# Sliding local attention beside a gated MLP: block 0's z2 from centred x, a 3 to 1 weight split, and later due times for the output

## The chip, the cores and the metric

The kernel runs on one core of a Trainium2 chip. A core has TensorE (PE in the profile, with its weight loads as PEld), VectorE (DVE), ScalarE (ACT), GpSimd (POOL) and SyncE (SP). SyncE and ScalarE issue most DMAs, each on its own queue. The metric is the device time of one execution, the median of the runs, in microseconds (us); lower is better.

## The reference

The input is x, 2048 tokens of 512 features in bf16. A layer norm without gain or bias gives xn, and the output is x + A(xn) + B(xn).

```python
# A: 32 heads of 16, each query sees 8 keys, 2 tokens apart, itself the last
qkv  = xn @ wqkv
attn = softmax(mask(q . k[pos - 2*w] * 0.25), over w = 0..7)
A    = (sum_w attn * v[pos - 2*w]) @ wo
# B: gated MLP that mixes tokens; w_in is 512 x 1792
z    = gelu(xn @ w_in)            # two halves of 896: z1 and z2
z2   = layernorm(z2)
g    = w_sp @ z2 + b_sp           # w_sp is 2048 x 2048, over tokens
B    = (z1 * g) @ w_out
```

## The kernel before

**A planner.** The kernel does not write instructions straight out. It adds tasks (`T` and `dma` call `Plan.add`, line 54), each with an engine, the buffers it reads and writes, a guessed duration and a name. `Plan.schedule` (line 95) then plays the tasks through on these guesses and so fixes one order per engine. Among the tasks that can start first it takes the one with the better priority and then the one added earlier; most of the attention's VectorE work has the lower priority `FILL`. A DMA is taken to last its bytes over a bandwidth, and to be usable a fixed latency later (`dma_lat`, 1700 ns, used at line 193). A task can have a margin: it is not taken before its inputs' planned end plus that margin. Output blocks have 1500 ns (line 983). The tasks then run on the chip in the planned order on each engine, with semaphore waits for what they depend on. The plan only sets the order; how long things take is up to the chip.

`plan.orders` (line 1010) writes part of the order by hand: in each list, the named tasks of an engine must start in this sequence.

**The head.** Tokens are in 16 blocks of 128. For a block, `ln_block` (line 594) takes statistics on VectorE (`bnst` line 598, `bnag` line 601), the inverse root of the variance on GpSimd (`rstd`, line 603), and normalises on VectorE (`norm`, line 605). The first four blocks are transposed by TensorE against an identity (`xTr`, line 620) and copied out of PSUM by ScalarE (`xTe`, lines 626 and 634); for block 0 VectorE copies the second half (`xTf`, line 630). Later blocks are transposed by a DMA (`xTd`, line 609). While x and the first weights are loading, TensorE runs matmuls on zeros (`warm` and `fill0`, line 570): nine of 512 columns, and later two of 320.

`z2_block` (line 777) multiplies one block with the second half of w_in, 448 columns at a time (`z2_b_hf`, line 785, four matmuls over the 512 features), and ScalarE takes the gelu and its row sums (`z2g`, line 790). These weights come in four DMAs (`ld_win_h`, line 541): `w_in2a` and `w_in2b` are the first and second 448 columns, each cut into two halves of the features, one on SyncE's queue and one on ScalarE's.

**The middle.** Per group of 512 tokens: Q and K (`qk_pair`, line 665, ScalarE's copy line 673), V to DRAM (line 647), the products of queries and shifted keys and their sums on VectorE (lines 689 and 694), a DMA transposition (line 706), sums within a head (714, 717) and the softmax. Meanwhile TensorE does z2 and z1 (line 802).

**The end.** TensorE forms g in 28 groups of 16 matmuls (`g_group`, line 908), with w_sp transposed by DMA (`ld_wT`, line 841). VectorE multiplies each by z1 (line 915), and between these does the attention's sum over values (`pv_pair`, lines 933, 937, 941), on V rows gathered by a DMA on ScalarE's queue (line 925). Each pair's result is transposed by a DMA on SyncE's queue (`OTd`, line 946). There are two pairs to a group of 512 tokens. `out_block` (line 956) fills a PSUM bank with x, adds the attention's product with wo (line 974) and the MLP's with w_out (line 978), and stores the result (copy line 987, DMA line 990).

Of the kernel before, what the change touches and what calls it, by code (L numbers as in the profile page):

```python
# [14 lines left out]
class Plan:  # L15
# [79 lines left out]
    def schedule(self, lookahead=64, slack=120.0, dma_bw=300.0, xbar_bw=190.0,  # L95
# [37 lines left out]
        while remaining:  # L133
# [52 lines left out]
            if t.dma is not None:  # L186
# [6 lines left out]
                t.end = max(xe, st + iss) + dma_lat  # L193
# [115 lines left out]
    warm=9,  # L309
    fill0=2,  # L310
# [4 lines left out]
def build_kernel(nc, A_x, A_wqkv, A_wo, B_x, B_w_in, B_w_sp, B_b_sp, B_w_out, out, report=False, sched_kw=None,  # L315
# [79 lines left out]
    with ExitStack() as es:  # L395
# [68 lines left out]
        R("xnT0a", "sb", [(off["xnT"] + dc * S, off["xnT"] + dc * S + 128) for dc in range(2)])  # L464
        R("xnT0b", "sb", [(off["xnT"] + dc * S, off["xnT"] + dc * S + 128) for dc in range(2, 4)])
# [5 lines left out]
        for nm, lo, hi, h0, h1 in (("w_in1", 0, FH, 0, 4), (("w_in2a", 0), FH, FH + HF, 0, 2),  # L471
                                   (("w_in2a", 1), FH, FH + HF, 2, 4), (("w_in2b", 0), FH + HF, 2 * FH, 0, 2),
                                   (("w_in2b", 1), FH + HF, 2 * FH, 2, 4)):
            R(nm, "sb", [(off["w_in"] + dc * 1792 + lo, off["w_in"] + dc * 1792 + hi) for dc in range(h0, h1)])
# [23 lines left out]
        def dma(eng, fn, nbytes, chan, reads=(), writes=(), name="", xbar=False, prio=None):  # L498
            return T(eng, fn, reads=tuple(reads), writes=tuple(writes), name=name, prio=prio,
                     dma=dict(chan=chan, nbytes=nbytes, xbar=xbar))  # L500
# [40 lines left out]
        def ld_win_h(nm, lo, n):  # L541
            for h in range(2):
                dma(("sp", "act")[h], (lambda h: lambda e: e.dma_start(
                    AC(off["w_in"] + lo + 2 * 1792 * h, [[1792, 2], [1, n]]),
                    B_w_in[256 * h: 256 * h + 256, lo: lo + n].rearrange("(c p) n -> p c n", p=128)))(h),
                    256 * n * 2, (nm, h), writes=[(nm, h)], name="ld%s_%d" % (nm, h))
# [3 lines left out]
        ld_win_h("w_in2a", FH, HF)  # L550
        ld_win_h("w_in2b", FH + HF, HF)
        ld_x(2, "sp")
        ld_x(3, "act")
        for which, eng in ((0, "sp"), (1, "sp")):
# [3 lines left out]
                512 * 512 * 2, ("wqk", which), reads=[("w_in2a", 0)],  # L558
                writes=[(("wq", "wk")[which], c) for c in range(4)],
                name="ld%s" % ("qk"[which]))  # L560
        for b in range(4, min(8, NB)):
            ld_x(b, "sp", after=[("w_in2a", 0)])
# [31 lines left out]
        def ln_block(b):  # L594
# [10 lines left out]
            T("dve", lambda v: v.tensor_scalar(A("xn", 512, 512 * sl), xin, Fv("mv", 1, 2 * b),  # L605
                                               Fv("rstd", 1, b), ALU.subtract, ALU.mult),
              reads=[("xin", xs_), ("mv", b), ("rstd", b)], writes=[("xn", sl)], est=400, name="norm%d" % b)
            if b >= XDMA:
                dma("sp", lambda e: e.dma_start_transpose(AC(off["xnT"] + 128 * b, [[S, 4], [1, 128]]),
                                                          A("xn", 512, 512 * sl)),  # L610
                    128 * 512 * 2, ("xT", sl), reads=[("xn", sl)], writes=[("xnT", b)], name="xTd%d" % b, xbar=True)
                return
            k = next_bank()
            k2 = next_bank() if b == 0 else k

            def tr(t):
                last = None
                for dc in range(4):
                    kk = k if dc < 2 else k2
                    last = t.matmul(ps[:, 512 * kk + 128 * dc: 512 * kk + 128 * dc + 128],  # L620
                                    A("xn", 128, 512 * sl + 128 * dc), ident, start=True, stop=True)
                return last
            T("pe", tr, reads=[("xn", sl), "ident"], writes=[("ps", k), ("ps", k2)], est=4 * c_mm(128),
              name="xTr%d" % b)
            if b == 0:
                T("act", lambda a: a.activation(AC(off["xnT"] + 128 * b, [[S, 2], [1, 128]]),  # L626
                                                ps[:, 512 * k: 512 * k + 256].rearrange("p (c n) -> p c n", c=2),
                                                ACTF.Copy),
                  reads=[("ps", k)], writes=["xnT0a"], est=c_act(256), name="xTe%d" % b)
                T("dve", lambda v: v.tensor_copy(AC(off["xnT"] + 2 * S + 128 * b, [[S, 2], [1, 128]]),  # L630
                                                 ps[:, 512 * k2 + 256: 512 * k2 + 512].rearrange("p (c n) -> p c n", c=2)),
                  reads=[("ps", k2)], writes=["xnT0b"], est=c_dve(256), name="xTf%d" % b)
            else:
                T("act", lambda a: a.activation(AC(off["xnT"] + 128 * b, [[S, 4], [1, 128]]),
                                                bank(k).rearrange("p (c n) -> p c n", c=4), ACTF.Copy),
                  reads=[("ps", k)], writes=[("xnT", b)], est=c_act(512), name="xTe%d" % b)
            if b == 0:
                filler(cfg["fill0"], "fill0", 160.0 * cfg["fill0"], reads=("zeros", ("xn", 0)), w=320)
# [138 lines left out]
        def z2_block(b):  # L777
            for hf in range(2):
# [3 lines left out]
                def mm(t, k=k, c0=c0):  # L782
                    last = None
                    for dc in range(4):
                        last = t.matmul(ps[:, 512 * k: 512 * k + HF], AC(off["xnT"] + dc * S + 128 * b, [[1, 128]]),  # L785
                                        AC(off["w_in"] + 1792 * dc + c0, [[1, HF]]), start=(dc == 0), stop=(dc == 3))
                    return last
                T("pe", mm, reads=[("xnT", b), (("w_in2a", "w_in2b")[hf], 0), (("w_in2a", "w_in2b")[hf], 1)], writes=[("ps", k)],
                  est=4 * c_mm(HF), name="z2_%d_%d" % (b, hf))
                T("act", (lambda k, hf: lambda a: a.activation(  # L790
                    A("z2", HF, FH * b + HF * hf), ps[:, 512 * k: 512 * k + HF], ACTF.Gelu_apprx_tanh,
                    accum_out=Fv("s1", 1, 2 * b + hf)))(k, hf),
# [276 lines left out]
```

## Time and profile before

| | us |
|---|---|
| median of 3 runs (lowest, highest) | 236.54 (236.46, 236.55) |
| profiled execution, its own time | 238.13 |
| span of that execution, first to last instruction | 236.3 |
| TensorE busy in the span | 230.9 (98%) |
| VectorE busy | 202.8 (86%) |
| ScalarE busy | 117.6 (50%) |
| GpSimd busy | 51.8 (22%) |

A line of the timeline has the start and the length in us, the engine, the source line and operation, what is written and read, how many instructions were merged, and in brackets the idle time before and who ended it. A q after an engine's name (SPq) means the issuing of a DMA, not its transfer. A line of the waits has who waited for whom, the total in us, how often, and the longest. A line of the chain of work has a start, a length and what ran. The view of one source line gives durations in ns and, for DMAs, the time from issue to landing in us.

### The profile page before, as it was taken

How to read it: one execution, taken by the hardware profiler on the slowest of the kernel's cores; microseconds unless marked ns; L12 is line 12 of the kernel's file. 1: busy time of each engine (PE TensorE's matmuls, PEld its weight loads, DVE VectorE, ACT ScalarE, POOL GpSimd, SP SyncE). 2: the span in 40 equal slices, each digit the busy share in tenths (PEclk: the TensorE clock that was granted, in tenths of full speed). 3: DMA queues.
4: the chain of work that ended last, by engine and by line, in shares of the span. 5: the costliest groups of instructions: out<-in, count | busy, mean ns of one | idle time of the engine just before them, and what ended most of it. 6: DMA issues, size and time to landing. Idle time of an engine off the chain costs nothing.

```text
span 236.3 us, 2933 instructions
## 1 busy us (share of the span) xinstructions
PE 230.9 (98%) x1094; PEld 109.9 (47%) x1094; DVE 202.8 (86%) x230; ACT 117.6 (50%) x227; POOL 51.8 (22%) x67
## 2 busy tenths in 40 slices
PE   8999999999999999999999999999999799999995
PEld 2454454554554444444444444444444344444553
DVE  4789969998989989997999991799999999999900
ACT  2798488988988978942012132134124134111441
POOL 4447963771690050001301000001000000000000
DMA  6999986290209899696549999999773959912132
GB/s 226 281 356 189 206 223 192 92 178 0 90 3 178 202 249 260 116 247 214 147 96 242 199 215 232 248 182 337 191 206 93 243 147 275 223 23 44 67 89 67
DMA packets 87021, 41.75 MB, mean 177 GB/s; under 512 B 66000, under 2 KB 85856, under 8 KB 87008
## 3 DMA queue, kind: packets, MB, share of 16 engines
q1 hardware_dynamic: 70928, 23.24, 48.4%
q10 hardware_dynamic: 14640, 14.13, 20.4%
q0 software_dynamic: 1440, 4.21, 6.6%
q8 instruction: 8, 0.13, 0.2%
q14 instruction: 5, 0.04, 0.0%
HBM read 20.05 MB, written 5.26 MB: 107 GB/s over the span
## 4 chain that ended last, share of the span: by engine, by line
DVE 50%; PE 31%; DMA 9%; POOL 5%; issue 2%; ACT 2%; DVEq 0%
DVE arena L689 11%; DVE arena L694 9%; DMA arena<-arena 9%; PE ps L908 9%; PE ps L978 6%; DVE arena L933 6%; DVE arena L937 4%; DVE arena L915 4%; POOL fpool L831 4%; PE ps L974 4%; PE ps L665 4%; PE ps L647 3%; PE ps L785 3%; DVE arena L834 2%; DVE arena L717 2%
## 5 line engine op out<-in xcount | busy, mean ns | idle before, releaser
L908 PE MATMUL ps<-arena 128*128 128x512 bf16 x448 | 97.5, 379 | 0.0
L908 PEld LDWEIGHTS ps<-arena 128*128 128x128 bf16 x448 | 43.9, 98 | 52.8 <-ACT ps L902 0.2
L902 ACT ACTIVATE ps<-arena 128x512 f32<-128x512 bf16 x28 | 16.5, 599 | 62.2 <-DVE arena L915 62.1
L933 DVE TENSOR_TENSOR arena<-arena 128x4096 bf16<-128x4096 bf16 x16 | 36.3, 2285 | 0.4
L689 DVE TENSOR_TENSOR arena<-arena 128x4096 bf16<-128x4096 bf16 x16 | 36.1, 2285 | 0.2
L937 DVE TENSOR_TENSOR arena<-arena 128x4096 bf16<-128x4096 bf16 (+1 forms) x16 | 28.1, 1754 | 0.3
L665 PE MATMUL ps<-arena 128*128 128x512 bf16 x128 | 28.3, 379 | 0.0
L694 DVE TENSOR_TENSOR arena<-arena 128x4096 bf16<-128x4096 bf16 x12 | 27.5, 2288 | 0.2
L978 PE MATMUL ps<-arena 128*128 128x512 bf16 (+2 forms) x119 | 27.0, 366 | 0.0
L785 PE MATMUL ps<-arena 128*128 128x448 bf16 x128 | 25.5, 353 | 0.2 <-DVE arena L630 0.2
L802 PE MATMUL ps<-arena 128*128 128x512 bf16 x112 | 24.3, 379 | 0.0
L665 PEld LDWEIGHTS ps<-arena 128*128 128x128 bf16 x128 | 14.5, 113 | 13.1
L915 DVE TENSOR_TENSOR arena<-ps,arena 128x512 bf16<-128x512 f32 x28 | 19.1, 680 | 0.0
L673 ACT ACTIVATE arena<-ps 128x1024 bf16<-128x1024 f32 x16 | 16.3, 1021 | 5.3 <-PE ps L665 4.9
L987 ACT ACTIVATE arena<-ps 128x512 bf16<-128x512 f32 (+1 forms) x16 | 9.4, 585 | 18.4 <-PE ps L978 17.0
L790 ACT ACTIVATE arena<-ps 128x448 bf16<-128x448 f32 x32 | 17.3, 542 | 2.4
L978 PEld LDWEIGHTS ps<-arena 128*128 128x128 bf16 x119 | 13.2, 113 | 11.3
L974 PE MATMUL ps<-arena 128*128 128x512 bf16 (+2 forms) x68 | 16.6, 366 | 1.6 <-DMA arena<-arena 1.6
L785 PEld LDWEIGHTS ps<-arena 128*128 128x128 bf16 x128 | 12.3, 98 | 12.0 <-ACT arena L626 0.7
L807 ACT ACTIVATE arena<-ps 128x512 bf16<-128x512 f32 x28 | 15.9, 595 | 3.2 <-PE ps L802 2.7
L802 PEld LDWEIGHTS ps<-arena 128*128 128x128 bf16 x112 | 10.9, 98 | 13.2
L679 POOL COPY arena<-arena 128x16 bf16<-128x16 bf16 x12 | 14.4, 1207 | 10.9 <-DVE arena L689 9.2
(61 smaller groups left out, 191.2 us busy)
## 6 DMA issues: line engine op xcount, KB each, us to landing
arena<-vscr ACTq DMA_DIRECT2D x8, 1152.0 KB, 7.5
arena<-in_A_x_dram ACTq DMA_DIRECT2D x17, 128.0 KB, 6.0
vscr<-arena POOLq DMA_DIRECT2D x16, 128.0 KB, 2.3
arena<-in_A_x_dram SPq DMA_DIRECT2D x15, 128.0 KB, 4.6
out_dram<-arena ACTq DMA_DIRECT2D x15, 128.0 KB, 1.9
arena<-in_A_wqkv_dram SPq DMA_DIRECT2D x3, 512.0 KB, 5.4
ascr<-arena POOLq DMA_DIRECT2D x4, 256.0 KB, 4.1
arena<-ascr POOLq DMA_DIRECT2D x4, 256.0 KB, 3.5
```

What stands on the lines that cost most here:

```text
L665: last = t.matmul(bank(k + which), AC(off["wqk"] + 1024 * dc + col0, [[4, 128]]), AC(off["xnT"] + dc * S + 512 * j, [[1, 512]]), start=(dc ...
L689: T("dve", lambda v: v.tensor_tensor(pbv, qb, kb, ALU.mult), reads=[("QT", c, j), ("KT", c, j), ("KTpad", c, j)], writes=[("pb", s_)], est ...
L694: T("dve", lambda v: v.tensor_tensor(A("pb", 4096, 4096 * a), A("pb", 4096, 4096 * a), A("pb", 4096, 4096 * b), ALU.add), reads=[("pb", b) ...
L785: last = t.matmul(ps[:, 512 * k: 512 * k + HF], AC(off["xnT"] + dc * S + 128 * b, [[1, 128]]), AC(off["w_in"] + 1792 * dc + c0, [[1, HF]]) ...
L790: T("act", (lambda k, hf: lambda a: a.activation(A("z2", HF, FH * b + HF * hf), ps[:, 512 * k: 512 * k + HF], ACTF.Gelu_apprx_tanh, accum_ ...
L802: lastm = t.matmul(bank(k), AC(off["w_in"] + 1792 * dc + 128 * fc, [[1, 128]]), AC(off["xnT"] + dc * S + 512 * j, [[1, 512]]), start=(dc = ...
L908: last = t.matmul(bank(k), AC(off["z2"] + FH * sh + 128 * fc, [[1, 128]]), AC(off["wT"] + WSL * r_ + sh * 512, [[1, 512]]), start=False, s ...
L915: T("dve", lambda v: v.tensor_tensor(uv, bank(k), uv, ALU.mult), reads=[("ps", k)], writes=[("z1T", fc, tc)], est=c_dve(512) + 20, name="u ...
L933: T("dve", (lambda iv, tv, av: lambda v: v.tensor_tensor(tv, iv, av, ALU.mult))(iv, tv, av), reads=[("attn", j), ("Ve", par)], writes=[("V ...
L937: T("dve", (lambda n: lambda v: v.tensor_tensor(AC(off["Vs"], [[4096, 2], [1, n]]), AC(off["Vs"], [[4096, 2], [1, n]]), AC(off["Vs"] + n, ...
L974: t.matmul(po, AC(off["OT"] + 512 * ot_pos(tb) + 128 * cc, [[1, 128]]), AC(off["wo"] + 512 * cc + c0, [[1, n]]), start=False, stop=False, ...
L978: last = t.matmul(po, AC(off["z1T"] + fc * S + t0, [[ts, 128]]), AC(off["w_out"] + 512 * fc + c0, [[1, n]]), start=False, stop=(fc == FC - ...
```

## The change

Block 0: VectorE only subtracts the mean from x, in two halves of 256 features (`ctr0`, `ctr1`). TensorE transposes the halves, ScalarE copies both out, and z2 of block 0 is computed from them in two steps of two matmuls each. The inverse root is applied later, as the scale of ScalarE's gelu. The normalised block 0, which Q, K, V and z1 still need, is now computed on GpSimd and transposed by a DMA on SyncE's queue.

Loads: `w_in2a` is cut 3 to 1 over the features, with three quarters on ScalarE's queue and one on SyncE's. x block 2 goes ahead of `w_in2b` on SyncE's queue. x blocks 4 and 5 now follow the Q and K weights, and these follow block 0's transposition.

Written orders: on VectorE the statistics of block 2 now come before the normalisation of block 1 (they came after); GpSimd gets a list. Warm-up matmuls go from nine to seven and the filler's from two to one.

Planner: a DMA can have a latency of its own, 3400 ns for the V rows and 3600 ns for the attention's transpositions (1700 before), and the margin of output blocks goes from 1500 to 2500 ns.

```diff
-                t.end = max(xe, st + iss) + dma_lat
+                t.end = max(xe, st + iss) + t.dma.get("lat", dma_lat)
...
-    warm=9,
-    fill0=2,
+    warm=7,
+    fill0=1,
...
-        def ld_win_h(nm, lo, n):
-            for h in range(2):
-                dma(("sp", "act")[h], (lambda h: lambda e: e.dma_start(
-                    AC(off["w_in"] + lo + 2 * 1792 * h, [[1792, 2], [1, n]]),
-                    B_w_in[256 * h: 256 * h + 256, lo: lo + n].rearrange("(c p) n -> p c n", p=128)))(h),
-                    256 * n * 2, (nm, h), writes=[(nm, h)], name="ld%s_%d" % (nm, h))
+        def ld_win_h(nm, lo, n, cut, h):
+            c0, c1 = (cut, 4) if h == 0 else (0, cut)
+            dma(("sp", "act")[h], lambda e: e.dma_start(
+                AC(off["w_in"] + lo + 1792 * c0, [[1792, c1 - c0], [1, n]]),
+                B_w_in[128 * c0: 128 * c1, lo: lo + n].rearrange("(c p) n -> p c n", p=128)),
+                128 * (c1 - c0) * n * 2, (nm, h), writes=[(nm, 1 - h)], name="ld%s_%d" % (nm, h))
...
-        ld_win_h("w_in2a", FH, HF)
-        ld_win_h("w_in2b", FH + HF, HF)
+        for h in range(2):
+            ld_win_h("w_in2a", FH, HF, 3, h)
         ld_x(2, "sp")
+        for h in range(2):
+            ld_win_h("w_in2b", FH + HF, HF, 2, h)
...
+            if b == 0:
+                for h in range(2):
+                    T("dve", (lambda h: lambda v: v.tensor_scalar(A("attn", 256, 256 * h), xin[:, 256 * h: 256 * h + 256],
+                                                                  Fv("mv", 1, 2 * b), None, ALU.subtract))(h),
+                      reads=[("xin", xs_), ("mv", b)], writes=[("xc", h)], est=270, name="ctr%d" % h)
+            T("pool" if b == 0 else "dve", lambda v: v.tensor_scalar(A("xn", 512, 512 * sl), xin, Fv("mv", 1, 2 * b),
                                                Fv("rstd", 1, b), ALU.subtract, ALU.mult),
...
-            if b >= XDMA:
+            if b >= XDMA or b == 0:
                 dma("sp", lambda e: e.dma_start_transpose(AC(off["xnT"] + 128 * b, [[S, 4], [1, 128]]),
...
+                    T("pe", trh, reads=[("xc", h), "ident"], writes=[("ps", k)], est=2 * c_mm(128), name="xTr0%d" % h)
+                    T("act", (lambda h, pt: lambda a: a.activation(A("attn", 256, 512 + 256 * h), pt, ACTF.Copy))(h, pt),
+                      reads=[("ps", k)], writes=[("xcT", h)], est=c_act(256), name="xTe0%d" % h)
...
-                    accum_out=Fv("s1", 1, 2 * b + hf)))(k, hf),
+                    scale=Fv("rstd", 1, 0) if b == 0 else 1.0, accum_out=Fv("s1", 1, 2 * b + hf)))(k, hf),
...
-                writes=[("Ve", par)], name="ldVe%d_%d" % (j, par), prio=FILL)
+                writes=[("Ve", par)], name="ldVe%d_%d" % (j, par), prio=FILL, lat=3400.0)
...
-                xbar=True)
+                xbar=True, lat=3600.0)
...
-                  margin=1500.0)
+                  margin=2500.0)
...
-            ["bnst0", "bnag0", "bnst1", "norm0", "bnag1", "xTf0", "norm1", "bnst2", "bnag2", "bnst3", "norm2", "bnag3",
+            ["bnst0", "bnag0", "ctr0", "ctr1", "bnst1", "bnag1", "bnst2", "norm1", "bnag2", "bnst3", "norm2", "bnag3",
              "norm3", "bnst4"],
-            ["warm", "xTr0", "fill0", "z2_0_0", "xTr1", "z2_0_1", "z2_1_0", "xTr2", "z2_1_1", "xTr3", "z2_2_0", "z2_2_1",
-             "z2_3_0", "z2_3_1"],
-            ["actprime", "ldw_in2a_1", "ldw_in2b_1", "ldx3", "xTe0", "xTe1", "z2g0_0", "z2g0_1", "xTe2", "z2g1_0", "xTe3", "z2g1_1"],
-            ["ldx2", "ldx4", "ldx5", "ldq", "ldk", "ldx6", "ldx7", "ldwv"],
+            ["warm", "xTr00", "xTr01", "fill0", "z2_0_0a", "z2_0_0b", "xTr1", "z2_0_1a", "z2_0_1b", "z2_1_0", "xTr2",
+             "z2_1_1", "xTr3", "z2_2_0", "z2_2_1", "z2_3_0", "z2_3_1"],
+            ["actprime", "ldw_in2a_1", "ldw_in2b_1", "ldx3", "xTe00", "xTe01", "xTe1", "z2g0_0", "z2g0_1", "xTe2", "z2g1_0",
+             "xTe3", "z2g1_1"],
+            ["rstd0", "norm0", "rstd1", "rstd2", "rstd3"],
+            ["ldx0", "ldx1", "ldw_in2a_0", "ldx2", "ldw_in2b_0", "xTd0", "ldq", "ldk", "ldx4", "ldx5", "ldx6", "ldx7",
+             "ldwv"],
```

## The prediction

> **What bounds the kernel now.** I began with the page's busy times.
>
> ```profile
> PE 230.9 (98%) x1094; PEld 109.9 (47%) x1094; DVE 202.8 (86%) x230; ACT 117.6 (50%) x227; POOL 51.8 (22%) x67
> ```
>
> TensorE (PE) is busy for 230.9 of 236.3 us and the work on it hardly changes. Time can only come from its start, from its idle stretches and from what follows its last matmul. The waits and the chain of work say where it is idle late.
>
> ```profile
> PE ps L974 <- DMA arena<-arena: 1.6, 1, 1.6
> ```
>
> ```profile
> 133.03 16.36 DMA arena<-arena
> ...
> 184.50 4.61 DMA arena<-arena
> 189.12 0.14 issue
> 189.25 1.02 PE ps L974 x4
> ```
>
> At 189.25 PE waits once for a transposition of attention output, issued at 184.50 when VectorE (DVE) had finished that pair, and landed 4.6 later. PE's previous group started its 16 matmuls at 184.03; at 0.2158 each (96 in 20.72 later in the chain) they end at 187.48, so 1.77 us are lost. There is no second such gap: from 10.46 to 233.68, the last matmul, PE stands still nowhere else. The last piece of VectorE's chain is as near, though. In the timeline of the end:
>
> ```profile
> 223.50 0.69 DVE L941 TENSOR_TENSOR arena<-arena 128x1024 bf16<-128x1024 bf16 x1
> 224.22 1.23 SPq L946 DMA_TRANSPOSE arena<-arena  x1
> ...
> 228.96 1.03 PE L974 MATMUL ps<-arena 128*128 128x512 bf16 x4
> ```
>
> Line 946 asked for this issue alone gives 3.9 us to landing, so 228.13. The output block that needs it starts at 228.96, in its turn. With 0.13 from landing to matmul (189.12 to 189.25) it could have started at 228.26: 0.70 us of slack, no more. The timeline of the head:
>
> ```profile
> 6.49 0.92 PE L785 MATMUL ps<-arena 128*128 128x448 bf16 x4 [0.19 <-DVE arena L630]
> 6.93 0.69 DVE L598 BATCH_NORM_STATS2 fpool<-arena 128x6 f32<-128x512 bf16 x1 [0.38 <-DMA arena<-in_A_x_dram]
> ...
> 7.25 0.39 PE L620 MATMUL ps<-arena 128*128 128x128 bf16 x4
> ...
> 8.33 0.49 PEld L785 LDWEIGHTS ps<-arena 128*128 128x128 bf16 x4 [0.37 <-ACT arena L634]
> ...
> 10.46 3.19 PE L785 MATMUL ps<-arena 128*128 128x448 bf16 x16
> ```
>
> Real work starts at 6.49; the transposition of block 1 at 7.25; block 1's z2 at 8.33; block 2's z2 at 10.46, after which PE never stops. VectorE's statistics of x block 2 wait for its load until 6.93. So 10.46 is the time to beat.
>
> **The change part by part, the head.** The sum is a difference in the span (236.29); the profiled execution took 238.13, 1.6 above the median of 236.54, so I subtract the difference from the median.
>
> Warm-up, nine to seven matmuls of 512 columns, and the filler, two to one: at 0.427 from start to start, two are 0.85 us, which PE would now idle through. The seventh ends its turn at about 4.14.
>
> Block 0's path: its mean is ready at 3.99 (line 601 starts 3.79, 0.20). The first centring is half of a 0.41 row, some 0.30, so 4.33; two matmuls of 128; ScalarE's copy of 256 (0.38) ends near 5.25, the second near 5.55. The inverse root (0.58) and the normalisation on VectorE (0.41) leave this path. z2 could start at 5.3 if the weights were there.
>
> Weights and x: the head's DMAs are served one after the other in issue order at some 350 GB/s. Landings, from issue plus time to landing: x0 3.0, x1 4.0, second half of the first weights (ScalarE's queue) 3.7, the other half 1.64 + 3.8 = 5.4, x3 6.1, x2 2.62 + 4.3 = 6.9, and the last half of the second weights 2.11 + 4.5 = 6.6, the slowest in line 543's view:
>
> ```profile
> L543 SPq DMA_DIRECT2D arena<-in_B_w_in_dram x2: 426/448/469, 1.6 to 2.1; - x2
> ...
> DMA to landing us min/median/max: 2.8/3.6/4.5
> ```
>
> Now count kilobytes in order. Until the first weights are complete, before: x0 128, weights 224, x1 128, 224, 224 = 928. After: 128, 336, 128, 224, 112 = 928. The split 3 to 1 moves nothing: 5.4. x2 is seventh now, at 128+336+128+224+112+128+128 = 1184 KB; before, the seventh, at 1180 KB, landed at 6.6. I take 6.5; were the queues to share evenly, with the shorter SyncE pieces running ahead, 5.8. Ends 5.8 and 6.6.
>
> VectorE's written order puts block 2's statistics ahead of block 1's normalisation, so this load is what everything queued on VectorE waits for, and PE behind it. Statistics 6.53; normalisation 0.64 later (4.05 to 4.69 is such a pair), 7.17 to 7.58; transposition of block 1 at 7.63 (0.05, as 5.10 to 5.16), against 7.25. Block 0's second z2 half, written after that, no longer fills PE before it; PE ends the first half by 7.0 even at four cold matmuls of 0.373 (448/512 of 0.427) from 5.5, and stands idle for 0.6 to 1.1. Block 1's z2 follows the transposition by 1.08 (7.25 to 8.33): 8.71. Then two z2 halves at 0.757 and two transpositions at 0.224: 10.67, against 10.46. Block 3's normalisation, on the same VectorE sequence, is done near 10.05 and no longer costs the 0.15 that PE idles at 10.23. **Head: 0.21 us lost**; between 0.5 gained (x2 at 5.8) and 0.3 lost.
>
> GpSimd gets block 0's normalisation between two inverse roots. No row shows it. Memsets on it grow by 0.78 ns a column (0.201 to 0.301 for 128 to 256), giving 0.5 us for 512; a 1-element power stretched to 2.68 at 16.49 beside a long VectorE product is the far end. I take 0.65, nearest the elementwise rows, as VectorE runs no such product before 16.47. Block 1's root then ends at 6.0, free until 7.17; at 2.68 it would cost 0.8.
> The Trainium skill, "GPSIMD Engine Reference", section "Engine selection", warns against elementwise work there, but calls one-input operations roughly line-rate; by its 1.2 GHz that is an estimate of 0.43 us, and the head's sum would be the same.
>
> SyncE now waits for that normalisation (5.35) before a DMA transposition (1.27 to 1.54 to issue); behind it queue the Q and K weights, x4 to x7 and the V weights. Q issues at about 7.0 instead of 6.33, K at 7.5; with the old 4.4 and 5.4 to landing 11.4 and 12.9, against needs at 13.7 and 14.6. Block 0's transposed copy (5.6 to 6.7 in the crowded rows) is there by 12.5. x4 to x7 come up to 5 us later, which delays VectorE's layer norms by 1 to 1.6. The cover is in SyncE's timeline:
>
> ```profile
> 121.63 11.36 SPq L841 DMA_TRANSPOSE arena<-in_B_w_sp_dram  x1
> 133.03 6.30 SPq L706 DMA_TRANSPOSE arena<-arena  x1
> ```
>
> The second starts only when the first is issued, though VectorE's input to it (124.57 and 127.38, two sums of 2.28) is ready at 129.66: 3.4 us of cover. Cost nothing; without it, all the lateness.
>
> The gelu's scale is an operand of the same instruction: nothing.
>
> **The margins.** The planner's assumed latency of the attention transposition rises by 1.9 us and the margin by 1.0: due times of output blocks move by 2.9. One group on PE is 16 x 0.2158 = 3.45. In the old plan's own due times block 5 could go 2.1 before PE came free for it, so 2.9 more puts it behind one more group: PE then arrives at 187.48 + 3.45 = 190.9, after 189.12. **1.77 us of idle time go.** The longer latency of the V loads (line 925) changes no order that I can see: VectorE's products never wait over 0.13 for them.
>
> **What is late next.** PE would end 1.77 - 0.21 = 1.56 earlier. But the last transposition follows VectorE, which is packed from 149.41 to 224.19; that start follows the DMA issued at 133.03, and this the one at 121.63, which PE's group ending 121.4 lets go. So VectorE shifts with the head, +0.21: issue at 224.43. Landing 3.9 after, as now, or 3.0 (the issue at 214.31). The slow one had an output store beside it, issued 225.04; that store now goes out 1.56 earlier and is over, so I take 3.0: landing 227.5, block at 227.6 instead of 228.96, **1.36 gained**. With 3.9 it is 0.5. 236.54 - 1.36 = 235.18, so 235.2.
>
> **A rule against it.** Matmuls of 512 columns start 0.427 apart in the warm-up, those of 448 columns 0.189 apart from 6.49 (16 in 3.03 from 10.46): the clock rises by some 5 us after the first one. With holes at 4.2 and 6.9 it may rise later. Eight z2 matmuls then cost 8 x 0.184 = 1.47 more.
> The Trainium skill, "TensorE: Matmul & The Clock Gate", section "What's actually happening", speaks against the shorter warm-up: full speed comes after a busy window of 3.4 us in a free-running grid. A missed window, half speed from 7.9 to 9.7, would be an estimate of 0.9 us, making 236.1.
>
> **Rivals.**
> A. Forecast: 235.2; its own range 234.9 to 236.1.
> B. The head gains as named: x2 lands at 5.8, 10.46 becomes 9.96. End: 0.70 + 0.87 (3.9 less 3.0) + 0.5 = 2.1 gained, 234.4. For it: the shorter pieces ahead; against: strict issue order so far.
> C. The plan leaves block 5 where it is: gap stays, head lost, 236.75. Against: 2.9 beats 2.1.
> D. Clock late, or GpSimd at 2.68: 0.8 to 1.5 more lost in the head, 236.0 to 236.6. For it: the row at 16.49, the holes; against: no long VectorE product near, the three runs within 0.09 us.
> E. **Slower**: the later layer norms push VectorE's plan so that the work after the 16.36 us transposition is written ahead of the product that now runs at 140.44 (2.28). VectorE then waits 8.9 instead of 6.7 at 149.41, and the last transposition comes 2.2 later: 236.54 + 2.2 - 1.36 = 237.4. In the old plan the transposition lands 1.3 after that product starts, so it decides once the plan's VectorE is late by more than that. For it: up to 1.6 of lateness; against: idle plan time before.
>
> **How the numbers follow.** A 0.45, B 0.17, C 0.08, D 0.12, E 0.13, unnamed 0.05. A measurement tells about 0.2% (0.47 us) from no change. Faster: A nearly whole, B, part of D: 0.62. Same: C, rest of D, A with 3.9: 0.13. Slower: E, unnamed, the worst of D: 0.25. Range 234.3 (B) to 237.0, with E's far end left out.
>
> **What would show it.** Right: the wait at line 974 gone from 189; VectorE's statistics of block 2 waiting on a load until about 6.5, and PE idle just before block 1's transposition at 7.6; a short wait for a transposition before the third last output block, near 227.6. Wrong: block 2's z2 starting before 10.2 (B), matmuls 0.37 apart after 7.6 (D), an idle stretch of VectorE over 8 us near 149 (E).

## The result, and the profile after

The changed kernel takes 239.36 us (median of 5, 238.75 to 245.39) against 236.54 for the kernel before (median of 5 beside it, 236.45 to 237.81). The ratio is 1.0125, 95% interval 1.009 to 1.016: slower, where 235.2 and a range up to 237.0 had been forecast. (Ratios leave disturbed executions out, so they need not equal the quotient of the two medians.) The profiled execution took 242.01 us with a span of 240.2; it is 2.65 above the median, so it shows more loss than the median one.

The page's busy times and the row of the granted clock:

```profile
PE 232.5 (97%) x1091; PEld 109.5 (46%) x1091; DVE 202.3 (84%) x230; ACT 116.5 (49%) x228; POOL 44.6 (19%) x68
...
PEclk9999999999999999999997999999999999999999
```

TensorE is busy 1.6 us longer than before (230.9) on the same work, and VectorE's work is the same. One slice, near 130 us, has a clock of 0.7 of full speed. The waits (who waited for whom, total us, how often, longest):

```profile
DVE fpool L601 <- DMA arena<-in_A_x_dram: 7.1, 4, 4.3
DVE arena L613 <- DMA arena<-arena: 5.5, 3, 3.9
...
PE ps L928 <- ACT ps L922: 2.1, 1, 2.1
...
PE ps L798 <- ACT arena L685: 0.8, 2, 0.5
PE ps L644 <- DVE arena L613: 0.6, 1, 0.6
```

The old wait of an output block for the attention's transposition (now line 994) is not among them. A new one is: a g group (line 928) stands 2.1 us for ScalarE to fill its PSUM bank. The timeline of the head, and below it four later places:

```profile
4.75 2.08 POOL L613 TENSOR_SCALAR arena<-arena,fpool 128x512 bf16<-128x512 bf16 x1
...
6.45 0.69 DVE L601 BATCH_NORM_STATS2 fpool<-arena 128x6 f32<-128x512 bf16 x1 [0.81 <-DMA arena<-in_A_x_dram]
...
6.86 1.27 SPq L618 DMA_TRANSPOSE arena<-arena  x1
7.42 0.41 DVE L613 TENSOR_SCALAR arena<-arena,fpool 128x512 bf16<-128x512 bf16 x1 [0.28 <-POOL fpool L606]
...
7.89 0.40 PE L644 MATMUL ps<-arena 128*128 128x128 bf16 x4 [0.60 <-DVE arena L613]
...
9.34 2.02 SPq L534 DMA_DIRECT2D arena<-in_A_x_dram  x4
...
11.07 3.19 PE L798 MATMUL ps<-arena 128*128 128x448 bf16 x16
...
14.58 0.69 DVE L601 BATCH_NORM_STATS2 fpool<-arena 128x6 f32<-128x512 bf16 x1 [4.33 <-DMA arena<-in_A_x_dram]
...
40.97 0.41 DVE L613 TENSOR_SCALAR arena<-arena,fpool 128x512 bf16<-128x512 bf16 x1 [3.88 <-DMA arena<-arena]
...
109.77 0.68 DVE L935 TENSOR_TENSOR arena<-ps,arena 128x512 bf16<-128x512 f32 x1
...
128.21 0.60 ACT L922 ACTIVATE ps<-arena 128x512 f32<-128x512 bf16 x1 [3.01 <-DVE arena L935]
128.87 6.39 PE L928 MATMUL ps<-arena 128*128 128x512 bf16 x21 [2.10 <-ACT ps L922]
```

Read it downwards. GpSimd needs 2.08 us for block 0's normalisation (4.75 to 6.83). SyncE waits for it, asks for block 0's transposition at 6.86, and so for x blocks 4 to 7 only at 9.34. VectorE then stands 4.33 us for block 4. At 40.97 it stands 3.88 more for the transposition of block 11. The first multiply by z1, which before was at 102.84, comes at 109.77: VectorE is 6.9 us late. ScalarE can fill a PSUM bank for a later g group only when VectorE's multiply has read it, so the fill at 128.21 comes late and TensorE stops. After the stop its clock is down; the windows around it (time, then PE busy and count, granted clock, DMA share, GB/s):

```profile
126.00:129.00 3.00, 0.90 (x5) 1.00 0.85 169
129.00:130.00 1.00, 1.00 (x4) 0.66 1.29 84
130.00:131.00 1.00, 1.00 (x4) 0.50 1.26 286
131.00:132.00 1.00, 1.00 (x4) 0.50 1.27 290
132.00:133.00 1.00, 1.00 (x5) 0.63 1.28 291
```

The table places the difference. Each column is the start of one kind of instruction in a profiled execution; "stop" is what TensorE loses among the g groups, from one matmul's start to the next, beyond the usual 0.2158 (2.27 for the idle 2.10 above). The last column is the number of 448-column matmuls of the head that ran at half speed (over 0.5 us each instead of 0.35).

| profiled execution | first Q matmul | first g | last g | last matmul | first multiply by z1 | stop | half speed in the head |
|---|---|---|---|---|---|---|---|
| before | 13.49 | 97.26 | 214.50 | 233.68 | 102.84 | 0 | 0 |
| after | 14.10 | 98.98 | 218.41 | 237.59 | 109.77 | 2.27 | 2 |
| before, again | 14.04 | 97.59 | 213.24 | 232.42 | 103.47 | 0.16 | 0 |
| before, made late on VectorE | 13.79 | 98.25 | 221.45 | 240.63 | 109.00 | 5.03 | 0 |
| before, x4 and x5 late | 13.42 | 97.19 | 212.71 | 231.89 | 106.74 | 0 | 0 |
| before, short warm-up | 15.57 | 99.13 | 214.60 | 233.78 | 104.72 | 0 | 9 |
| after, repaired | 13.62 | 97.18 | 212.65 | 231.83 | 102.62 | 0 | 0 |

Between the first two rows the last matmul moves by 3.91 us, as the span does (240.20 less 236.29). Of it 0.61 is in the head. 1.1 lies between Q and g, in two pauses of z2 that end with ScalarE's copies at 71.05 and 73.28 (line 685 above, whose idle time the waits give as 0.8). The g groups grow by 2.2: a stop of 2.27 and 1.7 of half-speed matmuls (the shortfalls 0.34, 0.50, 0.50 and 0.37 of the four windows) come in, and the old gap of 1.77 goes out. After the last g nothing changes.

### The profile page after: what moved, and what is told of

Its sections match the earlier page's. It is cut to its first block, busy times and chain, and to the rows that moved or that the text cites. A ratio compares the mean times of both kernels' runs of the same rounds, so it can differ in the third digit from the quotient of the medians.

```text
span 240.2 us, 2932 instructions
## 1 busy us (share of the span) xinstructions
PE 232.5 (97%) x1091; PEld 109.5 (46%) x1091; DVE 202.3 (84%) x230; ACT 116.5 (49%) x228; POOL 44.6 (19%) x68
## 4 chain that ended last, share of the span: by engine, by line
PE 45%; DVE 35%; DMA 8%; POOL 8%; issue 2%; SPq 1%; ACT 1%; DVEq 0%; POOLq 0%
PE ps L928 30%; DVE arena L701 12%; PE ps L998 10%; DVE arena L706 8%; PE ps L994 6%; POOL fpool L851 4%; DMA arena<-arena 4%; DMA arena<-in_A_x_dram 3%; DVE arena L854 3%; DVE arena L935 2%; DVE arena L729 1%; POOL fpool L606 1%; DMA vscr<-arena 1%; POOL arena L691 1%; DVE arena L726 1%
## 5 line engine op out<-in xcount | busy, mean ns | idle before, releaser
L928 PE MATMUL ps<-arena 128*128 128x512 bf16 x448 | 99.4, 384 | 2.1 <-ACT ps L922 2.1
L677 PE MATMUL ps<-arena 128*128 128x512 bf16 x128 | 28.3, 379 | 0.0
L798 PE MATMUL ps<-arena 128*128 128x448 bf16 x128 | 26.4, 356 | 1.5 <-ACT arena L685 0.8
L822 PE MATMUL ps<-arena 128*128 128x512 bf16 x112 | 24.3, 379 | 0.0
L677 PEld LDWEIGHTS ps<-arena 128*128 128x128 bf16 x128 | 14.5, 113 | 13.1
L810 ACT ACTIVATE arena<-ps 128x448 bf16<-128x448 f32 x30 | 16.1, 551 | 1.7
L601 DVE BATCH_NORM_STATS2 fpool<-arena 128x6 f32<-128x512 bf16 x16 | 10.6, 663 | 7.1 <-DMA arena<-in_A_x_dram 7.1
L827 ACT ACTIVATE arena<-ps 128x512 bf16<-128x512 f32 x28 | 15.4, 621 | 2.1 <-PE ps L822 1.8
```

Source lines behind the costliest of these rows:

```text
L677: last = t.matmul(bank(k + which), AC(off["wqk"] + 1024 * dc + col0, [[4, 128]]), AC(off["xnT"] + dc * S + 512 * j, [[1, 512]]), start=(dc ...
L798: last = t.matmul(ps[:, 512 * k: 512 * k + HF], st, AC(off["w_in"] + 1792 * dc + c0, [[1, HF]]), start=(dc == 0), stop=(dc == 3))
L822: lastm = t.matmul(bank(k), AC(off["w_in"] + 1792 * dc + 128 * fc, [[1, 128]]), AC(off["xnT"] + dc * S + 512 * j, [[1, 512]]), start=(dc = ...
L928: last = t.matmul(bank(k), AC(off["z2"] + FH * sh + 128 * fc, [[1, 128]]), AC(off["wT"] + WSL * r_ + sh * 512, [[1, 512]]), start=False, s ...
```

## The experiments

Times are medians; each ratio is to the kernel before measured on the same chip beside it, with its 95% interval. That kernel's medians there were 236.71, 237.13, 237.15, 236.88 and 237.36.

### Was the late gap worth anything?

**The planner's part alone**: the three numbers of the change in the kernel before.

```diff
-                  margin=1500.0)
+                  margin=2500.0)
-                xbar=True)
+                xbar=True, lat=3600.0)
-                ... name="ldVe%d_%d" % (j, par), prio=FILL)
+                ... name="ldVe%d_%d" % (j, par), prio=FILL, lat=3400.0)
```

> The kernel before with the planner's part of the change alone (the two latencies and the margin of 2500 ns). The prediction's step 'block 5 moves behind one more group' would make this about 1.4 us faster than before (235.1). Rival: read from the new plan's order, block 5 still follows block 6 directly and TensorE reaches it at the same time, only blocks 0, 1 and 4 move; then the wait at line 974 stays at 1.6 us and the time is 236.5, within 0.2%.

Measured: 237.52, ratio 1.0031 (1.0011 to 1.0052). On these times the plan moves blocks 0, 1 and 4, but leaves block 5 in its place; there was no wait at line 974 all the same. The interval lies above 1; the profiled execution is the quickest (236.50) and doesn't show what costs the 0.3%.

**Only the margin, and more of it**, which does put block 5 behind one more g group:

```diff
-                  margin=1500.0)
+                  margin=5000.0)
```

> The kernel before with the margin alone at 5000 ns, which does put block 5 behind one more group of matmuls. If the late wait is worth what the prediction said, 1.77 us of idle time go and the last transposition caps the gain: 235.2 (0.9 to 1.4 us faster). If something else replaces the wait at once, 236.5.

Measured: 236.56, ratio 0.999 (0.9974 to 1.0005). The gap is gone and the time is the same.

**The kernel before once more**, unchanged, to see its profile in another execution.

> The kernel before, unchanged, profiled once more. Theory: the prediction read a wait of 1.6 us at line 974 in an execution of 238.13 us, 1.6 above the median; it belongs to that execution and not to the kernel. Then an execution near 236.5 has a span near 234.7, the last input of that block lands before TensorE asks for it, and the wait is under 0.3 us. Rival: the wait is there in every execution and the 1.6 us are overhead of profiling: span 236.3 again, wait 1.6 again.

Measured: 237.34, ratio 1.0015 (0.9993 to 1.0037); the profiled execution took 236.87. All that TensorE waited for in it, and its timeline at the place of the old gap:

```profile
PE ps L570 <- DVE fpool L508: 1.2, 1, 1.2
PE ps L620 <- DVE arena L605: 0.7, 2, 0.5
PE ps L785 <- DVE arena L630: 0.5, 1, 0.5
```

```profile
185.83 2.32 PE L908 MATMUL ps<-arena 128*128 128x512 bf16 x10
187.99 1.03 PE L974 MATMUL ps<-arena 128*128 128x512 bf16 x4
```

Output block 5 follows the g group without a pause. The gap of 1.77 us belonged to the one execution that had been profiled. That one took 238.13, 1.59 above the median: the gap is about as long as what set it apart.

### The head alone

**The change without the planner's part** (latencies and margin as before).

> The change without the planner's part (latencies 1700, margin 1500). Theory 1 (VectorE falls some 6 us behind from the late x blocks and the crowded transpositions, and TensorE then stands still at the second g group): the stop of about 2.3 us near 126 stays, and the wait at line 974 may come back: 238.5 to 240.5. Rival (the planner's part is what costs): 236.7 to 237.2, since the head alone costs 0.6.

Measured: 241.37, ratio 1.0173 (1.0084 to 1.0262). The loss is there without the planner's part, so it comes from the head's. First multiply at 109.78, a stop of 1.85; and in this execution seven z2 matmuls at half speed between 8.28 and 10.7, with Q at 15.85.

**Is it the V rows?** In the changed kernel ScalarE issues the second load of V rows at 33.30 us, beside the transpositions of blocks 11 to 15; before, at 98.10. Here it waits for a later transposition:

```diff
+                reads=[...] + ([("pTd", 1)] if (j, par) == (0, 1) else []),
```

> The changed kernel with one load moved: the V rows of the first group's second pair are not fetched until the second group's product transposition has landed (after 76 us, as in the kernel before, where this load ran near 98). VectorE's written order is identical to the changed kernel's. Theory 1: the wait of 3.9 us at 40.97 for a crowded transposition shrinks to under 0.5, VectorE arrives 3.5 us earlier at the second g group, TensorE's stop of 2.3 us there is gone and with it the low clock: 235.4 to 236.6. Rival (the head and its normalisation on GpSimd make the whole difference): 239, unchanged.

Measured: 240.57, ratio 1.0127 (1.0069 to 1.0186). The wait at 41 shrank from 3.9 to 2.0, but others grew; the first multiply came at 110.10 and TensorE stopped for 2.23. That part of my theory fell.

### Does lateness alone stop TensorE?

**The kernel before, made late**: three memsets of 4096 columns on VectorE after the last layer norm, in memory that is overwritten later. Nothing else differs.

```diff
+            if j == NJ - 1:
+                for q in range(3):
+                    T("dve", (lambda q: lambda v: v.memset(AC(off["z1T"] + 4096 * q, [[1, 4096]]), 0.0))(q),
+                      reads=[("rstd", NB - 1)], writes=..., est=5, name="late%d" % q)
```

> The kernel before with three fills of 4096 columns (some 2.1 us each, 6.4 together, into a buffer not yet in use) on VectorE right after block 15's normalisation; nothing else in any engine's order differs. If lateness of VectorE at the g groups is by itself what stops TensorE, the first multiplication by z1 comes 6 us later than its 103.5, TensorE stops for 1.5 to 2.5 us near the eighth or ninth g group, and the time is 238 to 240.5. Rival (the g groups have room for it, and the stop came from the changed order or loads): within 0.5 of the kernel before.

Measured: 244.98, ratio 1.0335 (1.031 to 1.0361). Its waits and its timeline:

```profile
PE ps L913 <- ACT ps L907: 4.9, 1, 4.9
```

```profile
119.84 6.21 PE L913 MATMUL ps<-arena 128*128 128x512 bf16 x28
130.91 9.39 PE L913 MATMUL ps<-arena 128*128 128x512 bf16 x35 [4.87 <-ACT ps L907]
```

The memsets took 1.77 us each. The first multiply came at 109.00, and the same stop appeared, longer, with seven half-speed matmuls after it (besides it, an output block waited 1.1 us for its transposition). VectorE's lateness is enough by itself to stop TensorE.

**One step of the change alone**: x blocks 4 and 5 behind the Q and K weights in the kernel before. The first attempt kept VectorE's old order as a whole:

```diff
-            ["ldx2", "ldx4", "ldx5", "ldq", "ldk", "ldx6", "ldx7", "ldwv"],
+            ["ldx2", "ldq", "ldk", "ldx4", "ldx5", "ldx6", "ldx7", "ldwv"],
```

> The kernel before with one step of the change alone: x blocks 4 and 5 behind the Q and K weights on SyncE's queue, VectorE's order held as it is (the plan moves the second load of V rows on ScalarE ahead by itself). Theory (late x blocks make VectorE late, and TensorE then stops at the g groups): VectorE waits for x block 4 by 2 to 4 us in the head, the first multiply by z1 comes at 105 to 109 instead of 102.8, and the median rises by 0.3 to 1.5 us, with a stop of PE at the g groups where the multiply is past 107. Rival (the clock in the head and GpSimd carry the loss, the x blocks none): first multiply by 104, median within 0.3 us of before.

Measured: 240.75, ratio 1.0127 (1.0089 to 1.0165). This tells nothing of the step: the kept order has block 5's statistics ahead of block 3's normalisation, so TensorE itself stood for 3.06 us at 13.29. The second attempt exchanges those two.

> As e15, but with one exchange in VectorE's written order: block 3's normalisation stands ahead of block 5's statistics, so that TensorE does not wait in the head for the late x blocks itself (in e15 it stood idle for 3.06 us at 13.29 for that reason, which is more than the whole step is meant to tell). Theory (late x blocks make VectorE late, and TensorE pays for it 100 us later): no idle TensorE over 0.5 us near 13, first multiply by z1 at 105 to 109, median 0.5 to 2 us over before, with the loss at the g groups or at the attention's transposition. Rival (the 3.9 us of e15 were its own hole in the head, and the late x blocks cost nothing else): median within 0.4 us of before.

Measured: 236.52, ratio 0.996 (0.9935 to 0.9986). Its timeline:

```profile
5.37 0.92 SPq L555 DMA_DIRECT2D arena<-in_A_wqkv_dram  x2
...
6.33 1.94 SPq L533 DMA_DIRECT2D arena<-in_A_x_dram  x4
...
11.74 1.29 DVE L598 BATCH_NORM_STATS2 fpool<-arena 128x6 f32<-128x512 bf16 x2 [1.64 <-DMA arena<-in_A_x_dram]
...
106.74 0.68 DVE L915 TENSOR_TENSOR arena<-ps,arena 128x512 bf16<-128x512 f32 x1
```

The rival won. The x blocks are asked for at 6.33, three microseconds earlier than in the changed kernel, because block 0's DMA transposition, with its wait for GpSimd, does not stand ahead of them; x block 4 landed at 11.34, against 7.51 before and 14.56 in the changed kernel. VectorE is 3.9 us late at the first multiply (3.3 against the other execution of before), and TensorE never stops. So there is cover of that size, and this step by itself stays within it.

### Taking steps back from the changed kernel

**x4 and x5 ahead of block 0's transposition again.**

```diff
-            ..., "ldw_in2b_0", "xTd0", "ldq", "ldk", "ldx4", "ldx5", "ldx6", "ldx7",
+            ..., "ldw_in2b_0", "ldx4", "ldx5", "xTd0", "ldq", "ldk", "ldx6", "ldx7",
```

> The changed kernel with x blocks 4 and 5 put back ahead of block 0's DMA transposition and the Q and K weights on SyncE's queue. Theory 1 (VectorE's lateness): VectorE's wait of 4.3 us for x block 4 falls under 1, it reaches the g groups some 4 us earlier, TensorE's stop of 1.7 to 2.3 us at the sixth to eighth g group is gone: 236.4 to 237.4, with the head's loss of 0.6 left. Rival (normalisation on GpSimd and the idle head, with the clock): 238.8 or more.

Measured: 237.71, ratio 1.0055 (1.0014 to 1.0097). First multiply at 103.68, no stop at the g groups. Its own profiled execution (239.17) lost 1.55 in the head before block 1's transposition and 1.83 at 230.0, at line 994.

**The same with VectorE's order held as in the changed kernel**, since the plan had changed it too.

> The changed kernel with x blocks 4 and 5 ahead again, but with VectorE's order held to the changed kernel's own, and the same order on TensorE and ScalarE. Theory 1: VectorE waits under 2 us for x blocks in all, its first multiplication by z1 comes at 104 to 107 instead of 109.8, TensorE's stop is under 0.5: 236.8 to 237.8. Rival (the order written on VectorE, not its lateness, causes the stop): the stop of about 2 us stays, 239 or more.

Measured: 238.31, ratio 1.0055 (1.0024 to 1.0085). First multiply at 108.48, no stop over 0.2; but z2 ran slowly for long, with 16 matmuls at half speed until 13.1 and Q at 16.90:

```profile
8.32 3.43 PE L798 MATMUL ps<-arena 128*128 128x448 bf16 x8
...
16.90 1.46 PE L677 MATMUL ps<-arena 128*128 128x512 bf16 x6
```

Here 108.48 comes without a stop and in the row made late 109.00 with 5.0, because TensorE itself is late here. What tells the two apart is the distance from the first g matmul to the first multiply. It is 10.4 to 10.8 us in the four profiled executions that stop for over 1 us (changed, without the planner's part, V rows late, before made late), 8.0 here, and at most 9.5 in all fifteen without such a stop (before: 5.6 and 5.9).

**Block 0's normalisation on VectorE**, ahead of block 2's statistics; the rest as changed.

```diff
-            T("pool" if b == 0 else "dve", ... name="norm%d" % b)
+            T("dve", ... name="norm%d" % b)
-            [..., "bnst1", "bnag1", "bnst2", "norm1", ...
+            [..., "bnst1", "bnag1", "norm0", "bnst2", "norm1", ...
```

> The changed kernel with block 0's normalisation on VectorE (ahead of block 2's statistics) instead of GpSimd. Block 1's root ends at about 6.2 instead of 7.4 and SyncE's transposition goes out at 6.1 instead of 6.9. Theory 1: x block 4 still lands near 13.7, VectorE stays 3 us late, the stop shrinks by at most 0.8: 238 to 239.5. Rival (GpSimd's 2.1 us make the difference): under 237.

Measured: 236.62, ratio 1.0011 (0.9979 to 1.0043). This one step takes back the loss, with x4 and x5 still behind Q and K. SyncE's transposition goes out at 5.68 instead of 6.86, VectorE needs 0.37 us for it, the first multiply is at 104.37, Q at 13.61. But x block 4 landed only 1.5 us earlier (13.06 instead of 14.56), and VectorE still stood 3.53 us for it; what is gone is the wait near 41 and other later ones. VectorE's order differs in the middle as well, so what the step does on SyncE and what the new order does are not told apart by it.

**Both steps back, the V rows late, and block 1's normalisation ahead of block 2's statistics.** Measured twice.

> The changed kernel with three things put back: x blocks 4 and 5 ahead, block 0's normalisation on VectorE, and block 1's normalisation ahead of block 2's statistics; the V rows' second load is late again by the planner's own order. Block 1 is then transposed at about 6.8 and block 2's z2 starts at about 10.0 instead of 11.1 (10.46 before). Theory 1 and the head's reading together: no stop of TensorE after 11 us over 0.5, 235.6 to 236.4, faster than both. Rival: another wait at the g groups keeps it at 237 or above.

> The kernel of the run with three things put back, timed once more in more rounds: 0.2 to 0.4% faster than the kernel before, 235.9 to 236.3. Rival: the earlier 0.22% was chance, and the interval now includes no difference.

Measured: 236.18, ratio 0.9978 (0.9959 to 0.9996), and 237.01, ratio 1.001 (0.9977 to 1.0043). The second time six executions lie within 236.05 to 236.36 and six within 237.66 to 239.58; the profiled one, of the upper half, had nine half-speed matmuls in the head and Q at 15.03. The gain was not confirmed, and the slow heads pointed at the clock.

### The clock in the head

**The changed kernel with the long warm-up.**

```diff
-    warm=7,
-    fill0=1,
+    warm=9,
+    fill0=2,
```

> The changed kernel with nine warm-up matmuls and two fillers again; every engine's order is otherwise the same. The prediction's rival (the clock comes up late after the shorter warm-up) would make this 0.7 to 1.5 us faster than the changed kernel. Theory 1: the head waits for block 1's normalisation at 7.8 anyway, so nothing changes: 239 to 240.

Measured: 239.59, ratio 1.0083 (1.0055 to 1.0111). Restoring the warm-up alone brings nothing back that can be told: the median is that of the changed kernel, and the intervals of the two ratios overlap. Its profiled execution was its quickest (237.47): first multiply at 106.90, a stop of 0.29. VectorE's lateness varies between executions, and with it the stop.

**The kernel before with the short warm-up**, every order the same.

> The kernel before with warm-up seven and filler one, nothing else; every engine's order stays as it is. Theory of the late clock: in part of the executions z2's first four to eight matmuls run at half speed, 0.18 us each, Q starts 0.7 to 1.5 later than 13.49, and the median rises by 0.3 to 1.2 us over before. Rival (the warm-up doesn't matter where PE's later work is dense): same as before within 0.3 us, no half-speed matmul of 448 columns after 7.0.

Measured: 238.12, ratio 1.0034 (1.001 to 1.0057). Its head:

```profile
5.50 0.61 PE L620 MATMUL ps<-arena 128*128 128x128 bf16 x4 [1.15 <-DVE arena L605]
...
6.84 1.65 PE L785 MATMUL ps<-arena 128*128 128x448 bf16 x4 [0.46 <-DVE arena L630]
8.28 0.63 PE L620 MATMUL ps<-arena 128*128 128x128 bf16 x4
8.71 2.58 PE L785 MATMUL ps<-arena 128*128 128x448 bf16 x8
...
12.33 3.19 PE L785 MATMUL ps<-arena 128*128 128x448 bf16 x16
```

Four matmuls take 1.65 where they took 0.92, and eight 2.58 where they took 1.78: 1.53 us. With block 0's normalisation 0.34 later in this execution that makes the 1.87 by which block 2's z2 comes after 10.46. Over all profiled executions, the kernels with seven warm-ups had six or more half-speed matmuls in the head in six of nine; those with nine, at most two in all ten.

Two things are in this count. Here, and in the run with VectorE's order held, z2 starts at the warm-up's pace (one matmul every 0.37 us) and gains speed later; the row of the granted clock reads 1.00 all the while, so only the matmuls themselves show it. In the changed kernel without the planner's part and in that with the V rows late, z2 starts at full pace near 5.5, TensorE then stands 1.1 to 1.2 us for block 1's normalisation, and the granted clock falls. The first of these two, in windows as above:

```profile
7.00:8.00 1.00, 0.14 (x3) 1.00 0.00 0
8.00:9.00 1.00, 0.94 (x7) 0.66 0.65 131
9.00:10.00 1.00, 1.00 (x4) 0.50 0.48 35
10.00:11.00 1.00, 1.00 (x4) 0.50 0.66 225
11.00:12.00 1.00, 1.00 (x7) 0.63 1.09 385
```

That is the same 1.7 us as after the late stop of the changed kernel. In these two executions the late stops, 1.85 and 2.23 us, are not followed by a lower clock.

**The repaired kernel with the long warm-up**: the four steps of that kernel (x4 and x5 first, block 0 on VectorE, V rows late, block 1's normalisation first), and `warm=9, fill0=2`. Also measured twice.

> The changed kernel with the three undone steps of the earlier run (x blocks 4 and 5 first, block 0 normalised on VectorE, block 1 normalised ahead of block 2's statistics) and, besides, the warm-up of nine and the filler of two of the kernel before. Theory (two causes: VectorE's lateness, and a clock that comes up late after a short warm-up): both are out, at most two half-speed matmuls of 448 columns in the head, Q starts by 13.9, first multiply by z1 by 103.8, median 235.5 to 236.3, below the same kernel with seven warm-ups (237.01) and at or below before. Rival (the head's holes decide the clock, however long the warm-up): as with seven, four or more half-speed matmuls, Q at 14.5 to 15, median 236.6 to 237.4.

> The same kernel as e13, measured once more. Both theories that the earlier run left (it is a little faster than before; it is the same): if faster, the ratio is again under 1 with its whole interval; if the same, the interval holds 1 and the medians lie within 0.4 us.

Measured: 236.28 both times; ratios 0.998 (0.996 to 1.0001) and 0.9958 (0.9926 to 0.999). The waits of TensorE in the first:

```profile
PE ps L573 <- DVE fpool L509: 1.2, 1, 1.2
PE ps L798 <- DMA arena<-in_B_w_in_dram: 0.6, 1, 0.6
```

Of 24 executions 19 lie within 236.02 to 236.7. It is not slower than the kernel before, and the second time a little faster; its quickest execution gains only 0.2 us on the quickest of before beside it (236.02 and 236.22).

## Why the prediction was wrong, point by point

**The sum against one execution.** The step that failed first: "The sum is a difference in the span (236.29); the profiled execution took 238.13, 1.6 above the median of 236.54, so I subtract the difference from the median." The 1.77 us were to come off the median, yet they were what made that execution slower than the median. The second profile of before has no such gap and the margin alone gains nothing. The whole predicted gain hung on it. That block 5 goes behind one more group was right (the plan of the changed kernel does it), only there was nothing to gain.

**GpSimd at 0.65.** It took 2.08, between the bounds 0.5 and 2.68 and near the far one. I chose by memsets, which only write, and because no long VectorE product ran beside it; statistics of a block did. Its direct cost in this execution was small: block 1's transposition at 7.89 instead of 7.63, block 2's z2 at 11.07 instead of 10.67, so the head lost 0.61, not 0.21. The estimate from the Trainium skill, "GPSIMD Engine Reference", section "Engine selection" (one-input operations roughly line-rate, 0.43 us) is off by a factor of five here; the measurement decides. The rival with 2.68 had priced only the inverse root behind it.

**"x4 to x7 come up to 5 us later, which delays VectorE's layer norms by 1 to 1.6 … Cost nothing."** This step failed by the most: in the profiled execution it cost a stop of 2.27 us and 1.7 us of half speed, where nothing was forecast. x4 landed at 14.56 instead of 7.51, 7.0 later. Most of that is the new place in the queue; with the normalisation on VectorE it still landed at 13.06, so about 1.5 came from GpSimd, whose time went through SyncE's queue into every load behind it. VectorE stood 4.33 us for x4, and 3.88 for a DMA transposition at 40.97, of which I had thought nothing. Up to its first multiply it was idle for 19.5 us, against 12.2 before (13.7 with the normalisation on VectorE), and so 6.9 late. How the later of these waits follow from the loads, from GpSimd and from the plan's order is not shown. The cover had about the named size (3.4; 3.3 to 3.9 passed without a stop), which was luck, because it is in another place. It is not the DMA transposition at 133 that ends it but the g groups' PSUM banks, and before's own waits held a sign of it that I passed over:

```profile
PEld ps L908 <- ACT ps L902: 0.2, 1, 0.2
```

A weight load of a g group waited, briefly, for the bank's fill. When the cover ends, the cost can be more than the excess: in this execution the clock fell after the stop of 2.27 us, which took 1.7 more.

**The rule on the clock.** I gave a late clock 0.9 to 1.47 us, within a rival of 0.12. The short warm-up alone lifted the median of the kernel before from 236.88 to 238.12 (by the ratio 0.8 us), and its profiled head lost 1.53, near the upper value. So this belonged in the forecast. What I called the clock in the head was a pace: the row of the granted clock reads 1.00 there, in the warm-up too. The Trainium skill, "TensorE: Matmul & The Clock Gate", section "What's actually happening", has a free-running window, so that the same kernel differs from run to run. The one kernel that was profiled twice with seven warm-ups fits that, with 6 half-speed matmuls in one head and 9 in the other. The same section puts the drop after an idle window of about 3.4 us. Here it followed a stop of 2.27, and none followed stops of 1.85 and 2.23.

**What held.** The 3 to 1 split moved nothing (first weights complete at 5.65, forecast 5.4). x block 2 landed at 6.42 (6.5), though the working had a slip: before's seventh load landed at 1280 KB, not 1180, which by the same count gives about 6.4. PE's idle time moved to just before block 1's transposition (0.60, forecast 0.6 to 1.1). Q and K's weights landed at 12.68 and 14.18, 1.3 later than forecast for GpSimd's reason (11.18 and 12.68 with the normalisation on VectorE); Q waited for none. Rival E, slower by VectorE's plan at 149, ended on the right side with another mechanism.

**What stays open.** How the 2.8 us of the median divide between VectorE's lateness and the clock. Both vary between executions, and restoring the warm-up alone left the median where it was, while one step on VectorE alone took most of the loss back. The profiled execution, 2.65 above the median, can't settle the division, and the kernel's other executions were not profiled. The median one (239.36) has a mean granted clock of 0.992, by which some 1.9 us are lost; one of nearly the same time (239.34) has 1.000. A lowered clock goes with block 0's normalisation on GpSimd: of 42 executions of the six kernels that have it there, 17 have a mean clock of 0.993 or less; of 56 with it on VectorE and the rest of the change kept in whole or in part, none. So that step probably cost time in two ways, by lateness and by holes that lower the clock, and their shares are not shown.

## What to carry to other kernels

Before costing a stall, ask whether the profiled execution is the median: if it is slower by about the length of the stall, the stall is not there to be won. Follow a slow instruction through every queue that waits for it: 1.4 us more than priced, on an idle engine, made loads 1.5 us late for another one and left holes on the bounding engine. Two steps that each use up the same cover may cost little alone and much together (with either x4 and x5 or the normalisation put back, the ratio is 1.0055 or 1.0011; with neither, 1.0125), so sum the lateness per engine and compare it once with what the bounding engine can bear.

## What the runs showed of the hardware

- A GpSimd `tensor_scalar` of 128x512 bf16 took 2.08 us in all six profiles that have it (VectorE: 0.37 to 0.49).
- After a stop of 2.27 us in dense work TensorE ran at half speed for about 3.4 us (129.3 to 132.7). That is 1.7 us of lost time, 0.7% of the span, as the mean clock of 0.993 says. After stops of 1.85 and 2.23 us in two other profiles the clock stayed at 1.00; in the heads of these two it fell for 3.4 us after holes of 1.1 and 1.2, and in the run with x4 and x5 first a hole of 1.4 there brought no fall.
- With seven warm-up matmuls the heads of nine profiles had 0 to 16 half-speed matmuls, with nine at most 2. Where the pace had not yet risen, the row of the granted clock read 1.00 all the same.
